# Squared-ReLU attention with a mixture-of-depths layer behind it: the table that orders all instructions is drawn anew

## The chip, the core and the metric

The kernel runs on one core of a Trainium2 chip. The metric is device time in microseconds (us) of one execution; lower is better.

## What is computed

For 8 batches, 12 heads, 448 tokens and head dimension 64, attention without softmax, and on its output a layer in which only 128 tokens of each batch pass through a two-matrix network:

```
scores = (1/sqrt(64)) * q @ k^T
attn   = max(scores, 0)^2 / 448
x      = attn @ v                      # as [8, 448, 768]
score  = x @ w_gate                    # one number a token
top    = the 128 tokens of a batch with the largest score
h      = max(x[top] @ w1, 0)           # 768 -> 1024
y      = h @ w2                        # 1024 -> 768
out    = x;  out[top] = x[top] + sigmoid(score[top]) * y
```

Inputs and output are float32 in DRAM; the matmuls run in bf16.

## The kernel before

**Units.** The attention of a batch is cut into three units of four heads; unit u belongs to batch u // 3, so there are 24 units, 0 to 23. Each unit has seven chunks c of 64 key rows. The second layer goes batch by batch, 0 to 7.

**The order is a table.** The kernel is written as short steps, each a function that issues one to 28 instructions. A string, ORDER (from line 518), lists some 1280 steps by name and numbers; a loop calls them in that order (the lines behind `with tc.manual_schedule()`). Every engine keeps its own queue and runs its instructions in the order in which they were issued; between engines, semaphores hold an instruction until what it reads is there and what it overwrites is free. So the table sets the order on each engine. An engine whose next instruction has to wait holds all that stands behind it in its own queue. A scheduling program drew the table up; it is not part of the kernel.

**Attention steps.** L,i,b,hh,j0,j1 (line 99) loads part of q, k or v (i = 0, 1, 2) of batch b from DRAM, for one half hh of the heads, converting to bf16, and is issued by POOL. There are three buffers for each of q, k and v, used by batches in turn. Batch 0 is loaded in parts (j0 to j1) and, for its first two head pairs, through float32 tiles (qf and kf, line 95) that C turns into bf16. T,u,i (229) transposes unit u's q or k on PE; TE,u copies both from PSUM into qkT. T0, TE0, SH, RH and QH are the same for unit 0 in halves. S,u,c (292) is four matmuls that make the scores of a chunk; R,u,c is the ReLU out of PSUM into a_sb, of which nearly all run on ACT (167 at line 114); Q,u,g (305) squares a group of chunks on DVE; V,u,c (313) is four matmuls that multiply with v. X,u scales the unit's result into xT_sb, on ACT or DVE.

**Steps of the second layer, for batch b.** G and CE make token scores, BC and RK compare every score with every other, CS and RC add up ranks, HOT and SEL turn ranks into a list of tokens, SE writes that list (idx). XR transposes x back on PE and XE evicts it into rows; for batches 5 and 6 XD (430) does this with DMA transposes that SP issues, each as soon as its unit's X is done. ST,b (434) stores rows to DRAM. GA,b (440) gathers the chosen tokens from there, once ST,b has landed; XT and XTE transpose them. For batches 0 and 7 XO and XOE pick them by matmul instead, and GA's rows are used only at the end. GS and SG make the gate. H,b,f (487) and HE are the first matrix, Y (499) and YE (507) the second with the final sum into the tile fo (two buffers), FI,b (512) scatters fo to DRAM. W,0 and W,1 load the two weight matrices.

**Where an engine is chosen.** The last letter of TE, R, X, XE, XTE, XOE, HE and C names it, A for ACT and D for DVE; `put` (line 112) issues the eviction there, so many rows of the profile share lines 114 (ACT), 116, 118 and 120 (DVE).

**POOL's queue.** POOL issues every load of a batch, the stores, gathers and scatters. P,u (192) is a one-element copy of unit u's qkT: it holds POOL until that unit is transposed, so that loads behind it wait until a buffer is free. GA holds POOL until the list is there, FI until fo is. N is a tiny memset ahead of some gathers and scatters. SP's queue holds the XD steps alone, in the middle of the program.

**Fillers.** WU (127) and WS (136) are matmuls on a tile of ones whose results nobody reads.

Of the kernel before, what the change touches and what calls it, by code (L numbers as in the profile page):

```python
# [20 lines left out]
def kernel(  # L21
# [497 lines left out]
    Z,9 Z,7 Z,3 Z,4 Z,6 Z,1 Z,2 L,1,0,1,2,4 L,0,0,1,2,4 L,1,0,0,2,4 C,0,0,A C,1,0,A L,0,0,0,2,4 WU,10,7,3 T0,0,0,4  # L519
    T0,1,0,5 L,1,1,1,0,6 TE0,0,0,4,A C,0,1,D L,0,0,0,4,6 TE0,1,0,5,A WU,1,7,3 T0,0,1,6 C,1,1,D Z,8 L,1,0,0,4,6 Z,10  # L520
    TE0,0,1,6,A WG WU,3,7,3 SH,1,0,0 L,1,0,1,4,6 T0,1,1,4 SH,0,0,1 L,0,0,1,4,6 TE0,1,1,4,D SH,2,0,2 SH,3,0,3
    RH,0,0,1,D RH,1,0,0,A L,0,1,0,0,6 WS,1,6 SH,0,1,4 RH,2,0,2,A RH,3,0,3,D T,1,0,6 L,0,1,1,0,6 RH,0,1,4,A S,0,4,0
    T,1,1,7 L,1,1,0,0,6 R,0,4,0,A S,0,5,2 TE,1,2,6,D S,0,6,4 L,2,0,1,0,2 R,0,5,2,A SH,3,1,0 L,2,0,0,0,2 RH,3,1,0,D
    R,0,6,4,A WU,2,1,3 S,1,0,2 L,2,0,1,2,4 QH,1,0,2 WS,1,6 S,1,1,0 R,1,0,2,A QH,0,0,2 WS,1,6 SH,2,1,4 L,2,0,0,2,4
    RH,2,1,4,D R,1,1,0,A WU,2,7,3 S,1,2,2 Q,0,2,3 T,2,0,6 R,1,2,2,A S,1,3,4 S,1,4,0 T,2,1,7 R,1,3,4,A Z,5 SH,1,1,2
    TE,2,2,6,D R,1,4,0,A WU,1,3,4 S,1,5,4 R,1,5,4,A RH,1,1,2,D P,2 WU,2,3,3 S,1,6,0 L,0,2,1,0,6 QH,1,1,2 WS,2,6
    S,2,0,2 R,1,6,0,A L,2,0,1,4,6 S,2,1,4 QH,0,1,2 T,3,0,6 R,2,0,2,A Q,1,0,3 WU,2,7,3 T,3,1,7 R,2,1,4,A S,2,2,0
    S,2,3,2 TE,3,2,6,D R,2,2,0,A V,0,0,4,1,0 V,0,1,4,0,0 R,2,3,2,A S,2,4,0 Q,2,0,3 P,3 L,2,0,0,4,6 T,4,0,6 T,4,1,7
    R,2,4,0,A L,0,2,0,0,6 S,2,5,2 V,0,2,4,0,0 TE,4,2,6,D L,1,2,1,0,6 R,2,5,2,A S,2,6,0 V,0,3,4,0,0 V,0,4,4,0,0
    L,1,2,0,0,6 V,0,5,4,0,0 R,2,6,0,A V,0,6,4,0,1 Q,1,1,4 S,3,0,2 L,2,1,1,0,6 T,5,0,6 R,3,0,2,A S,3,1,0 L,2,1,0,0,6  # L530
    T,5,1,7 R,3,1,0,A S,3,2,2 TE,5,2,6,D R,3,2,2,A S,3,3,0 Q,2,1,4 P,5 R,3,3,0,A W,1,6,8 S,3,4,2 V,1,0,6,1,0
    V,1,1,6,0,0 W,0,4,6 V,1,2,6,0,0 X,0,2,4,A V,1,3,6,0,0 V,1,4,6,0,0 V,1,5,6,0,0 L,0,3,1,0,6 S,3,5,0 R,3,4,2,A
    V,1,6,6,0,1 Q,3,0,3 V,2,0,4,1,0 V,2,1,4,0,0 V,2,2,4,0,0 R,3,5,0,A V,2,3,4,0,0 S,3,6,2 X,1,2,6,D R,3,6,2,A S,4,0,0
# [158 lines left out]
```

## Time and profile before

| | |
|---|---|
| three runs | 213.47, 213.60, 213.68 us; median 213.6 |
| the profiled execution | 215.22 us |
| its span, first to last instruction | 213.1 us |
| mean granted TensorE clock | 0.968 |
| PE busy | 193.6 us (91%), 3177 matmuls |
| DVE busy | 170.8 us (80%) |
| ACT busy | 164.9 us (77%) |
| POOL busy | 91.7 us (43%) |
| DMA | 37.89 MB in 34335 packets, mean 178 GB/s |

The profile is one execution, some 1.6 us longer than the median of the runs. In its rows a line number and tile names stand for a step: `L292 PE MATMUL psum<-qkT` is S, `L114 ACT ACTIVATE a_sb<-psum` is R. In the order of time the first column is the start, the second the duration, both in us from the span's start; what stands in brackets is how long the engine had been idle and what ended that. "issue" there means that nothing the profile shows was waited for. A DMA's row has the median time from its issue to its landing.

### The profile page before, as it was taken

How to read it: one execution, taken by the hardware profiler on the slowest of the kernel's cores; microseconds unless marked ns; L12 is line 12 of the kernel's file. 1: busy time of each engine (PE TensorE's matmuls, PEld its weight loads, DVE VectorE, ACT ScalarE, POOL GpSimd, SP SyncE). 2: the span in 40 equal slices, each digit the busy share in tenths (PEclk: the TensorE clock that was granted, in tenths of full speed). 3: DMA queues.
4: the chain of work that ended last, by engine and by line, in shares of the span. 5: the costliest groups of instructions: out<-in, count | busy, mean ns of one | idle time of the engine just before them, and what ended most of it. 6: DMA issues, size and time to landing. Idle time of an engine off the chain costs nothing.

```text
span 213.1 us, 7252 instructions
## 1 busy us (share of the span) xinstructions
PE 193.6 (91%) x3177; PEld 123.9 (58%) x3177; DVE 170.8 (80%) x263; ACT 164.9 (77%) x209; POOL 91.7 (43%) x130
## 2 busy tenths in 40 slices
PE   6889979999999999999799999989599699999970
PEld 2545555556776557656466546755356475698940
DVE  1489999998999989969799998998369956985340
ACT  2989999999989988789799999989459678541100
POOL 7953671350667281625174297061070028035121
PEclk9999999999999999999999999999769969999996
DMA  5999999999499999999999959999989946629411
GB/s 152 141 179 202 151 184 205 209 282 195 49 307 217 278 143 183 340 170 139 187 288 195 179 95 141 162 127 155 285 117 264 103 80 154 218 27 343 118 77 74
DMA packets 34335, 37.89 MB, mean 178 GB/s; under 512 B 8960, under 2 KB 29440, under 8 KB 34304
## 3 DMA queue, kind: packets, MB, share of 16 engines
q0 software_dynamic: 26352, 34.94, 87.2%
q1 hardware_dynamic: 7632, 2.04, 11.1%
q10 hardware_dynamic: 320, 0.46, 0.8%
q8 instruction: 25, 0.41, 0.7%
q14 instruction: 6, 0.05, 0.1%
HBM read 42.47 MB, written 14.16 MB: 266 GB/s over the span
## 4 chain that ended last, share of the span: by engine, by line
PE 41%; DMA 21%; ACT 17%; issue 9%; POOL 8%; DVE 1%; POOLq 1%; ACTq 0%
ACT a_sb L114 15%; PE psum L292 10%; DMA v_sb<-in_v_dram 9%; PE psum L313 9%; DMA out_dram<-rows 7%; PE psum L487 6%; PE psum L229 5%; DMA k_sb<-in_k_dram 5%; PE psum L499 4%; POOL k_sb L99 2%; POOL q_sb L99 2%; PE psum L343 2%; PE psum L416 2%; PE psum L354 1%; ACT xT_sb L114 1%
## 5 line engine op out<-in xcount | busy, mean ns | idle before, releaser
L114 ACT ACTIVATE a_sb<-psum 128x896 bf16<-128x896 f32 (+1 forms) x167 | 142.2, 926 | 15.5 <-PE psum L292 13.2
L305 DVE TENSOR_TENSOR a_sb<-a_sb 128x2688 bf16<-128x2688 bf16 (+3 forms) x49 | 83.4, 1712 | 0.6 <-ACT a_sb L114 0.6
L292 PE MATMUL psum<-qkT 64*64 64x448 bf16 x656 | 60.2, 371 | 2.4 <-ACT a_sb L114 2.0
L313 PE MATMUL psum<-a_sb,v_sb 64*64 64x448 bf16 x672 | 45.6, 361 | 2.9 <-issue 2.4
L292 PEld LDWEIGHTS <-qkT 64*64 64x64 bf16 x656 | 21.1, 105 | 21.4 <-issue 12.3
L118 DVE COPY qkT<-psum 128x1792 bf16<-128x1792 bf16 (+1 forms) x24 | 25.6, 1068 | 9.1 <-PE psum L229 7.7
L440 POOL DMA_INDIRECT xe<-out_dram,idx x8 | 14.5, 1810 | 42.6 <-DVE idx L412 40.2
L313 PEld LDWEIGHTS <-v_sb 64*64 64x64 bf16 x672 | 20.8, 109 | 14.5 <-issue 5.5
L192 POOL COPY pace<-qkT 1x1 bf16<-1x1 bf16 x18 | 11.7, 650 | 36.7 <-DVE qkT L118 36.7
L487 PE MATMUL psum<-xeT,w_sb 128*128 128x128 bf16 x384 | 26.9, 223 | 0.0
L499 PE MATMUL psum<-w_sb,hT 128*128 128x384 bf16 x128 | 26.8, 328 | 0.0
L487 PEld LDWEIGHTS <-w_sb 128*128 128x128 bf16 x384 | 22.7, 99 | 2.6 <-issue 2.5
L434 POOL DMA_DIRECT2D out_dram<-rows x16 | 10.4, 654 | 21.7 <-DVE rows L118 16.1
L499 PEld LDWEIGHTS <-hT 128*128 128x128 bf16 x128 | 11.1, 97 | 9.5 <-issue 4.7
L512 POOL DMA_INDIRECT out_dram<-fo,idx x8 | 10.5, 1311 | 10.6 <-DVE fo L507 7.1
L114 ACT ACTIVATE xT_sb<-psum 128x896 bf16<-128x896 f32 x14 | 13.1, 935 | 2.4 <-PE psum L313 2.4
L229 PE MATMUL psum<-ident,k_sb 128*64 128x128 bf16 x322 | 13.2, 220 | 1.4 <-DMA k_sb<-in_k_dram 1.3
L99 POOL DMA_DIRECT2D v_sb<-in_v_dram x20 | 13.1, 667 | 3.2 <-DMA k_sb<-in_k_dram 2.1
L229 PE MATMUL psum<-ident,q_sb 128*64 128x128 bf16 x322 | 13.5, 224 | 0.9 <-DMA q_sb<-in_q_dram 0.9
L229 PEld LDWEIGHTS <-q_sb 128*64 128x64 bf16 x322 | 9.9, 111 | 7.0 <-issue 6.0
L507 DVE SCALAR_TENSOR_TENSOR fo<-psum,g,xe 128x384 f32<-128x384 f32 x16 | 9.7, 615 | 4.8 <-ACT g L483 2.0
L120 DVE TENSOR_SCALAR xT_sb<-psum 128x896 bf16<-128x896 f32 x10 | 10.9, 1088 | 2.9 <-PE psum L313 2.6
(84 smaller groups left out, 205.4 us busy)
## 6 DMA issues: line engine op xcount, KB each, us to landing
out_dram<-rows POOLq DMA_DIRECT2D x8, 768.0 KB, 6.6
k_sb<-in_k_dram POOLq DMA_DIRECT2D x14, 336.0 KB, 7.4
q_sb<-in_q_dram POOLq DMA_DIRECT2D x14, 336.0 KB, 8.5
v_sb<-in_v_dram POOLq DMA_DIRECT2D x14, 336.0 KB, 9.0
out_dram<-rows POOLq DMA_DIRECT2D x8, 576.0 KB, 7.1
w_sb<-in_moe_w_dram POOLq DMA_DIRECT2D x4, 384.0 KB, 8.5
w_sb<-in_moe_w_dram POOLq DMA_DIRECT2D x3, 512.0 KB, 8.1
v_sb<-in_v_dram POOLq DMA_DIRECT2D x6, 112.0 KB, 7.7
```

Of the source, the lines that this page charges most:

```text
L99: nc.gpsimd.dma_start(out=qkv_sb[i][b % NBUF][64 * hh:64 * hh + 64, j0:j1], in_=srcs[i][b, NJ * hh + j0:NJ * hh + j1].rearrange("h (p c) d ...
L114: nc.scalar.activation(out=out_, in_=in_, func=func or AF.Copy, scale=scale)
L118: nc.vector.tensor_copy(out=out_, in_=in_)
L120: nc.vector.tensor_scalar(out=out_, in0=in_, scalar1=scale, scalar2=None, op0=ALU.mult)
L192: nc.gpsimd.tensor_copy(out=pace, in_=qkT[u][0:1, 1, 1, NC - 1, 63:64])
L229: nc.tensor.matmul(out=psum16[64 * j2:64 * j2 + 64, at, c * 128:(c + 1) * 128], lhsT=t[:, 2 * w + j2, c, :], rhs=ident, is_transpose=True, ...
L292: nc.tensor.matmul(out=psum[64 * hh:64 * hh + 64, at + j2, :S].rearrange("x (c p) -> x c p", c=NC), lhsT=sb[rows, hh, 1, c, :], rhs=sb[row ...
L305: nc.vector.tensor_tensor(out=a, in0=a, in1=a, op=ALU.mult)
L313: nc.tensor.matmul(out=psum[64 * j2:64 * j2 + 64, at + hh, :S], lhsT=qkv_sb[2][b % NBUF][rows, 2 * w + j2, c, :], rhs=a_sb[u, g][rows, i, ...
L440: inst = nc.gpsimd.indirect_dma_start(out=self.xe, out_offset=None, in_=out[0:self.b + 1].rearrange("b s d -> (b s) d"), in_offset=bass.In ...
L487: nc.tensor.matmul(out=psum[:, at, sub * CAP:(sub + 1) * CAP], lhsT=w1_sb[:, m, f * 128:(f + 1) * 128], rhs=self.xeT[:, m, :], start=(sub ...
L499: nc.tensor.matmul(out=psum[:, at, 0:384], lhsT=self.hT[:, f, :], rhs=w2_sb[:, f, half * 384:half * 384 + 384], start=bool(first), stop=bo ...
```

## The change

ORDER alone is replaced: 1284 steps become 1280. All functions, tiles and buffers stay, and so do all steps of computation, loads, stores, gathers and scatters. What differs is the order of steps, the PSUM banks that they use, the engine of some evictions, and fillers: N stands four times instead of seven, WU makes 28 matmuls instead of 29, WS 52 instead of 24. TE0 goes from three on ACT and one on DVE to four on DVE, HE from seven on ACT and nine on DVE to 13 and 3, X from 14 and 10 to 16 and 8.

Two lines of the table before, and those that hold the same steps after (XD,5 of batch 5 and what stands around it):

```diff
-    R,17,4,2,A V,15,6,4,0,1 S,17,5,0 XT,3,5 L,0,7,1,0,6 X,15,2,6,D R,17,5,0,A Y,2,0,6,4,0,0
-    Y,2,0,7,4,0,1 S,17,6,2 R,17,6,2,A S,18,0,0 XTE,3,5,D XD,5,0,0 T,19,0,6 YE,2,0,4,D T,19,1,7 R,18,0,0,A S,18,1,2
...
+    V,15,3,4,0,0 S,17,6,2 V,15,4,4,0,0 V,15,5,4,0,0 R,17,6,2,A XT,3,6 XE,4,1,7,D S,18,0,0 V,15,6,4,0,1 XTE,3,6,D
+    R,18,0,0,A S,18,1,2 X,15,2,4,D T,19,0,6 R,18,1,2,A T,19,1,7 S,18,2,0 XD,5,0,0 TE,19,2,6,D V,16,0,4,1,0
```

**ACT, the start of the program.** Before, from the casts C of batch 0 on (q_sb and k_sb; qkT is TE0, a_sb of 448 is RH, of 896 R):

```order
L114 ACTIVATE q_sb_83<-qf 128x448
L114 ACTIVATE k_sb_86<-kf 128x448
L114 ACTIVATE qkT<-psum 64x7x2x64 x3
L114 ACTIVATE a_sb<-psum 128x448 x3
L114 ACTIVATE a_sb<-psum 128x896 x21
```

After, the same place:

```order
L114 ACTIVATE k_sb_86<-kf 128x448
L114 ACTIVATE q_sb_83<-qf 128x448
L114 ACTIVATE k_sb_86<-kf 128x448
L114 ACTIVATE a_sb<-psum 128x448 x2
L114 ACTIVATE a_sb<-psum 128x896 x28
```

The three TE0 have left ACT, a cast has come, one RH has left, and 28 R steps instead of 21 stand ahead of the first X.

**POOL, from GA,3 to the v load of batch 7.** In the names v_sb_89, q_sb_83 and k_sb_86 are the buffers of batch 6, q_sb_84, k_sb_87 and v_sb_90 those of batch 7; rows of xe are GA, of out_dram from rows ST,4, of out_dram from fo FI (896x768 is FI,1), and pace from qkT is P. Before:

```order
L440 DMA xe<-out_dram,idx 128x768
L205 MEMSET pace 1x1
L512 DMA out_dram<-fo,idx 896x768
L192 COPY pace<-qkT 1x1
L99 DMA q_sb_84<-in_q_dram 64x6x448
L192 COPY pace<-qkT 1x1
L99 DMA k_sb_87<-in_k_dram 64x6x448 x2
L99 DMA v_sb_89<-in_v_dram 64x6x448
L99 DMA q_sb_84<-in_q_dram 64x6x448
L434 DMA out_dram<-rows 64x4x768
L434 DMA out_dram<-rows 64x3x768
```

After:

```order
L440 DMA xe<-out_dram,idx 128x768
L99 DMA v_sb_89<-in_v_dram 64x6x448
L99 DMA q_sb_84<-in_q_dram 64x6x448
L99 DMA v_sb_89<-in_v_dram 64x6x448
L192 COPY pace<-qkT 1x1
L99 DMA k_sb_87<-in_k_dram 64x6x448 x2
L434 DMA out_dram<-rows 64x3x768
L434 DMA out_dram<-rows 64x4x768
L512 DMA out_dram<-fo,idx 896x768
```

FI,1 has moved from right behind GA,3 to behind ST,4. Two loads that stood behind P,18 (the last P here), one of v for batch 6 and one of q for batch 7, now stand ahead of it. The first q load of batch 7 now goes out ahead of GA,3, and a v load of batch 6 that went out ahead of it now follows it. All these loads are of the same size.

**ACT, the end of the attention.** Before, from the last but one pair of R steps on (xT_sb is X, g is SG, rows is XE,7):

```order
L114 ACTIVATE a_sb<-psum 128x896 x2
L114 ACTIVATE xT_sb_93<-psum 128x2x448
L114 ACTIVATE a_sb<-psum 128x896
L483 ACTIVATE g<-psum 128x1
L114 ACTIVATE rows<-psum 128x768 x3
```

After:

```order
L114 ACTIVATE a_sb<-psum 128x896 x4
L114 ACTIVATE xT_sb_93<-psum 128x2x448
L114 ACTIVATE a_sb<-psum 128x896 x2
L114 ACTIVATE xT_sb_93<-psum 128x2x448 x2
L114 ACTIVATE rows<-psum 128x768 x3
```

X,22 and X,23 now both stand behind the last R step on ACT; before, X,22 stood ahead of the last R and X,23 on DVE.

More of the change, by code (lines that the diff above doesn't have):

```diff
@@ L518 @@
     ORDER = """
[L519 to L533, printed above, removed]
@@ new lines @@
+    L,1,0,0,4,6 T0,1,0,5 TE0,0,0,4,D L,0,0,0,4,6 C,0,1,A TE0,1,0,5,D C,1,1,A L,0,1,0,0,6 WU,2,7,3 T0,0,1,4 TE0,0,1,4,D
+    WU,1,7,1 T0,1,1,5 L,0,0,1,4,6 SH,1,0,0 TE0,1,1,5,D SH,0,0,1 SH,2,0,2 L,1,0,1,4,6 RH,0,0,1,D RH,1,0,0,A WS,1,6
+    T,1,0,6 RH,2,0,2,A L,2,0,1,0,2 SH,3,0,3 S,0,4,0 S,0,5,4 RH,3,0,3,D L,0,1,1,0,6 R,0,4,0,A T,1,1,7 L,1,1,0,0,6
+    SH,3,1,2 TE,1,2,6,D R,0,5,4,A S,0,6,0 SH,2,1,3 L,2,0,0,0,2 R,0,6,0,A RH,2,1,3,D S,1,0,4 L,1,1,1,0,6 Z,5 R,1,0,4,A
+    L,2,0,1,4,6 WS,4,6 S,1,1,0 RH,3,1,2,D R,1,1,0,A QH,1,1,2 WS,4,6 S,1,2,2 S,1,3,4 T,2,0,6 Q,0,2,3 R,1,2,2,A S,1,4,0
@@ new lines @@
+    V,4,1,6,0,0 Q,5,1,4 R,6,1,2,A G,0,4,5,0,0 S,6,2,0 V,4,2,6,0,0 V,4,3,6,0,0 R,6,2,0,A G,0,5,5,0,1 S,6,3,2
+    V,4,4,6,0,0 V,4,5,6,0,0 V,4,6,6,0,1 R,6,3,2,A S,6,4,0 CE,0,5 X,4,2,6,D T,7,0,4 R,6,4,0,A T,7,1,5 S,6,5,2
+    TE,7,2,4,D BC,0,6 R,6,5,2,A S,6,6,0 RK,0,3,6 R,6,6,0,A V,5,0,4,1,0 P,7 RK,0,2,6 W,1,4,6 V,5,1,4,0,0 S,7,0,2
+    RK,0,1,6 V,5,2,4,0,0 V,5,3,4,0,0 R,7,0,2,A W,1,0,2 RK,0,0,6 V,5,4,4,0,0 S,7,1,0 V,5,5,4,0,0 L,2,2,0,0,6 Q,6,1,4
+    V,5,6,4,0,1 R,7,1,0,A S,7,2,2 T,8,0,6 X,5,2,4,A T,8,1,7 S,7,3,0 R,7,2,2,A TE,8,2,6,D CS,0,4 XR,1,3,5 R,7,3,0,A
@@ new lines @@
+    XR,2,0,7 R,10,4,2,A XE,2,1,5,D G,2,1,4,0,0 S,10,5,0 XR,2,3,6 R,10,5,0,A XR,2,2,5 XE,2,3,6,D G,2,2,4,0,0
+    G,2,3,4,0,0 G,2,4,4,0,0 G,2,5,4,0,1 S,10,6,2 CE,2,4 XE,2,2,5,D R,10,6,2,A WU,2,1,4 XT,1,6 S,11,0,0 XTE,1,6,D
+    S,11,1,4 S,11,2,2 R,11,0,0,A XE,2,0,7,D H,1,0,6,0 Q,10,1,4 H,1,1,6,1 R,11,1,4,A ST,2,1 H,1,2,6,2 H,1,3,6,3 ST,2,0
+    R,11,2,2,A H,1,4,4,0 S,11,3,0 P,11 L,0,5,1,0,6 HE,1,0,6,A BC,2,5 Q,10,0,3 R,11,3,0,A H,1,5,4,1 P,10 L,2,4,1,0,6
+    S,11,4,2 T,12,0,6 R,11,4,2,A T,12,1,7 RK,2,3,5 RK,2,2,5 S,11,5,0 TE,12,2,6,D H,1,6,4,2 R,11,5,0,A S,11,6,2
@@ new lines @@
+    BC,3,6 S,15,1,2 R,15,0,0,A HE,2,0,7,D T,16,0,4 T,16,1,5 RK,3,3,6 R,15,1,2,A RK,3,2,6 S,15,2,0 RK,3,1,6 H,2,4,7,0
+    R,15,2,0,A RK,3,0,6 S,15,3,2 H,2,5,7,1 TE,16,2,4,D R,15,3,2,A H,2,6,7,2 S,15,4,0 GS,2,6 R,15,4,0,A H,2,7,7,3
+    Q,14,1,4 P,16 S,15,5,2 L,1,6,1,0,6 V,13,0,4,1,0 V,13,1,4,0,0 R,15,5,2,A S,15,6,0 L,0,6,0,0,6 V,13,2,4,0,0
+    V,13,3,4,0,0 V,13,4,4,0,0 SG,2,6 R,15,6,0,A V,13,5,4,0,0 L,0,6,1,0,6 S,16,0,2 HE,2,1,7,D CS,3,6 V,13,6,4,0,1
+    R,16,0,2,A S,16,1,0 RC,3,6 X,13,2,4,D T,17,0,6 R,16,1,0,A T,17,1,7 HOT,3 S,16,2,2 V,14,0,4,1,0 TE,17,2,6,D
@@ new lines @@
+    V,14,1,4,0,0 R,16,2,2,A V,14,2,4,0,0 S,16,3,0 V,14,3,4,0,0 V,14,4,4,0,0 R,16,3,0,A Q,15,0,3 S,16,4,2 P,17
+    V,14,5,4,0,0 L,0,7,0,0,6 SEL,3,6 R,16,4,2,A Y,2,0,0,7,1,0 S,16,5,0 Y,2,0,1,7,0,0 V,14,6,4,0,1 SE,3,6 R,16,5,0,A
+    Q,15,1,4 S,16,6,2 GA,3 Y,2,1,0,6,1,0 Y,2,1,1,6,0,0 Y,2,0,2,7,0,0 R,16,6,2,A Y,2,0,3,7,0,0 S,17,0,0 Y,2,1,2,6,0,0
+    Y,2,1,3,6,0,0 R,17,0,0,A Y,2,0,4,7,0,0 Y,2,0,5,7,0,0 Q,16,1,4 L,2,6,0,0,6 Y,2,0,6,7,0,0 Y,2,0,7,7,0,1
+    Y,2,1,4,6,0,0 X,14,2,4,A S,17,1,0 L,0,7,1,0,6 S,17,2,2 Y,2,1,5,6,0,0 R,17,1,0,A L,2,6,1,0,6 T,18,0,4 T,18,1,5
@@ L639 @@
+    Y,7,0,2,4,0,0 Y,6,0,4,6,0,0 Y,6,0,5,6,0,0 Y,6,0,6,6,0,0 Y,6,0,7,6,0,1 Y,7,0,3,4,0,0 Y,7,1,0,5,1,0 YE,6,0,6,D
+    Y,7,0,4,4,0,0 Y,7,0,5,4,0,0 Y,7,0,6,4,0,0 GS,7,7 N FI,6 Y,7,0,7,4,0,1 Y,7,1,1,5,0,0 SG,7,7 Y,7,1,2,5,0,0
+    YE,7,0,4,D Y,7,1,3,5,0,0 Y,7,1,4,5,0,0 Y,7,1,5,5,0,0 Y,7,1,6,5,0,0 Y,7,1,7,5,0,1 YE,7,1,5,D N FI,7
     """
```

193 lines of the change are left out of this document (89 added, 104 removed).

## The prediction

> **What bounds the kernel now.** I read the page first, then the stretches of the span that its slices suggested, then the order of time where an engine stood still, and the DMA view of those places last. In the stretches each engine's busy time stands with its instruction count, then the granted TensorE clock and the DMA share:
>
> ```profile
> 21.00:50.80 29.80, 27.31 (x490) 16.10 (x491) 29.08 (x34) 29.69 (x38) 12.68 (x19) 1.00 1.17 205
> 50.80:130.70 79.90, 78.01 (x1363) 49.88 (x1356) 73.53 (x100) 72.15 (x92) 41.53 (x53) 1.00 1.05 196
> 130.70:150.00 19.30, 18.66 (x339) 12.45 (x339) 17.87 (x25) 18.20 (x24) 5.85 (x9) 1.00 1.43 151
> 150.00:160.00 10.00, 7.52 (x107) 4.17 (x105) 4.66 (x8) 5.14 (x7) 4.05 (x4) 0.66 1.03 195
> ...
> 175.70:184.10 8.40, 8.40 (x128) 4.94 (x128) 6.51 (x15) 7.67 (x10) 4.48 (x5) 1.00 0.83 232
> 184.10:206.60 22.50, 22.40 (x338) 18.27 (x330) 13.37 (x33) 3.89 (x8) 6.69 (x11) 1.00 0.44 122
> ```
>
> The columns are PE, PEld, DVE, ACT, POOL. From 21 to 50.8 us ACT is the bound (29.69 of 29.8). To 150 three engines share it: PE, DVE and ACT are each busy over 90%. From 184.1 to 206.6 PE alone works through the experts of the last batches (22.40 of 22.5). A last eviction, a scatter and its landing follow. One place stands out: from 150 to 160 ACT worked 5.14 of 10 us and the clock fell to 0.66. The order of time shows what happened, on PE and then on ACT:
>
> ```profile
> 149.86 0.21 PE L343 MATMUL psum<-wg,xT_sb 128*128 128x1 bf16 x3
> 152.56 0.54 PE L343 MATMUL psum<-wg,xT_sb 128*128 128x1 bf16 x15 [2.48 <-issue]
> 167.57 1.29 PE L313 MATMUL psum<-a_sb,v_sb 64*64 64x448 bf16 x21
> 170.64 0.38 PE L313 MATMUL psum<-a_sb,v_sb 64*64 64x448 bf16 x3 [1.77 <-issue]
> ...
> 153.66 1.97 ACT L114 ACTIVATE a_sb<-psum 128x896 bf16<-128x896 f32 x2 [2.73 <-PE psum L292]
> 156.27 0.92 ACT L114 ACTIVATE a_sb<-psum 128x896 bf16<-128x896 f32 x1 [0.64 <-PE psum L292]
> 157.70 0.92 ACT L114 ACTIVATE a_sb<-psum 128x896 bf16<-128x896 f32 x1 [0.52 <-PE psum L292]
> 159.46 4.16 ACT L114 ACTIVATE a_sb<-psum 128x896 bf16<-128x896 f32 x5 [0.84 <-PE psum L292]
> 171.06 0.92 ACT L114 ACTIVATE xT_sb<-psum 128x896 bf16<-128x896 f32 x1 [1.86 <-PE psum L313]
> ...
> 178.20 1.73 ACT L114 ACTIVATE a_sb<-psum 128x896 bf16<-128x896 f32 x2 [0.69 <-PE psum L292]
> ```
>
> PE twice stopped for "issue", that is, for nothing that the profile shows, and both times in the middle of a step: three matmuls into a G step of four, and one into a V step of four, whose data the first had already found. No data wait does that. ACT's idle time behind the first stop is 2.73 + 0.64 + 0.52 + 0.84 = 4.7 us, behind the second at least 1.86 + 0.69 = 2.6 us: 7.3 us in all. The DMA view explains the stops. Its first row is of the whole run, the second of 150 to 151.5 us, then median landing times of 80 to 120 us, and of 127 to 150 us:
>
> ```profile
> q8 instruction: 25, 0.41, 0.7%
> ...
> q8 instruction: 1, 0.02, 4.5%
> ...
> v_sb<-in_v_dram POOLq DMA_DIRECT2D x5, 336.0 KB, 8.7
> ...
> v_sb<-in_v_dram POOLq DMA_DIRECT2D x2, 336.0 KB, 13.0
> rows<-xT_sb SPq DMA_TRANSPOSE x6, 12.3
> out_dram<-fo,idx POOLq DMA_INDIRECT x1, 13.7
> ```
>
> PE's instructions come by DMA. The page counts 3177 matmuls and as many weight loads; over 25 packets that is 254 instructions each. The view of 140.4 to 150 us has no q8 row. In those 9.6 us PE ran, at the 678 instructions of 19.3 us above, some 337, more than a packet holds; a packet came in the next 1.5 us and PE went on. So PE ran dry, because its packet stood behind the transposes, loads, stores and scatter that took 12 to 14 us to land there. [...]
>
> **The change, part by part.** Work is the same; only order, banks and a few evictions' engines differ. All terms are against the profiled execution.
>
> *The head.* The rows are PE's first transposes, the cast of q's second half behind its landing, ACT's and DVE's first evictions to qkT, and the first double-width R:
>
> ```profile
> 5.91 0.58 PE L258 MATMUL psum<-ident,q_sb 128*64 128x128 bf16 x7 [1.45 <-ACT q_sb L114]
> 6.73 0.39 DVE L118 CAST q_sb<-qf 128x448 bf16<-128x448 f32 x1 [4.87 <-DMA qf<-in_q_dram]
> 6.52 2.65 ACT L114 ACTIVATE qkT<-psum 64x896 bf16<-64x896 bf16 x3 [0.20 <-PE psum L258]
> 9.28 0.63 DVE L118 COPY qkT<-psum 64x896 bf16<-64x896 bf16 x1 [1.18 <-PE psum L258]
> 11.55 4.98 ACT L114 ACTIVATE a_sb<-psum 128x896 bf16<-128x896 f32 x6 [0.63 <-PE psum L292]
> ```
>
> Three TE0, 2.65 us on ACT, go to DVE at 0.63 each, 1.9 us. The first two start near 6.4 as before and end near 7.6 instead of 8.3; the second half's casts (now on ACT, from 6.73) let the other two end near 9.2 instead of 9.9. Two RH instead of three stand on ACT ahead of its R steps, and S,0,4 is ready near 9.8: the first R comes near 10.3 instead of 11.55. Then ACT has R steps queued until unit 1, whose k half is landed by then. Up to 50.8 us ACT is the bound, so the lead stays. I take -1.1 us (0 to -1.4; 0 if unit 1's transposes still wait for their k loads).
>
> *The middle, 50.8 to 184.* Between R,6,6 and R,23,6 ACT gets two HE more (8 for 6) and DVE two fewer.
>
> ```profile
> L116 DVE TENSOR_SCALAR hT<-psum 128x512 bf16<-128x512 f32 x9 | 6.1, 687 | 4.7 <-PE psum L487 4.7
> L114 ACT ACTIVATE hT<-psum 128x512 bf16<-128x512 f32 x7 | 4.2, 600 | 4.9 <-PE psum L487 4.8
> ```
>
> That is 2 x 0.60 = +1.2 us on ACT and 2 x 0.69 = -1.4 on DVE. Each is busy about 90% there, so it costs between -1.4 and +1.2; I take +0.6, since ACT is what the late R steps wait for. Loads and T steps move against each other by one or two R in both directions; there I take 0, with 1.0 either way.
>
> *The congested stretch, 127 to 175.* POOL's rows show the burst in order of time; the last two rows are an X eviction and the transposes (XD) that SP issues as soon as it is done:
>
> ```profile
> 125.08 1.83 POOL L512 DMA_INDIRECT out_dram<-fo,idx  x1 [0.23 <-issue]
> 127.04 0.69 POOL L99 DMA_DIRECT2D q_sb<-in_q_dram  x1
> 131.39 0.69 POOL L99 DMA_DIRECT2D q_sb<-in_q_dram  x1
> 139.97 1.27 POOL L434 DMA_DIRECT2D out_dram<-rows  x2 [7.89 <-DVE rows L118]
> 142.59 2.07 POOL L512 DMA_INDIRECT out_dram<-fo,idx  x1 [0.30 <-issue]
> ...
> 158.07 1.09 DVE L120 TENSOR_SCALAR xT_sb<-psum 128x896 bf16<-128x896 f32 x1 [1.84 <-PE psum L313]
> 159.19 15.31 SPq L430 DMA_TRANSPOSE rows<-xT_sb  x6
> ```
>
> 158.07 + 1.09 = 159.16, and SP issues at 159.19: XD goes when X is done. Before, FI,1 (the 125.08) sits ahead of five loads that go out from 127.0 to 132.1. After, FI,1 stands behind ST,4, and three of the five loads go right behind GA,3 without waiting for P,18: about 1.5 us earlier. X,15 follows R,18,0 instead of R,17,4, X,16 R,18,4 instead of R,18,2, X,17 R,19,4 instead of R,19,3; with R steps of some 0.85 us (4.98 for six) the transposes go 2.6, 1.7 and 0.9 us later. ST,4 and the v load go 1 to 3 us later too. What went into the queues in 15.6 us (127.0 to 142.6) thus takes about 19. Counted along PE's order, its packet falls due at the same step as before, at S,19,2, with 3 to 4 us less ahead of it. It was late by the 2.48 us that PE stood still. So the stop should vanish or shrink to some tenths, and the clock stay up: I take -4.2 of the 4.7 us (0 to -4.7). At the second stop the same transfers are ahead (two ST,5, a v load, XD,6), now with FI,2 among them; ST,5 waits for the later XD,5, so one packet may pass ahead of them and the next not. I take half, -1.3 us (+1 to -2.6).
>
> [...]
>
> *The tail.* The rows: V steps, an XT, an X on ACT and the last X on DVE.
>
> ```profile
> 180.80 1.50 PE L313 MATMUL psum<-a_sb,v_sb 64*64 64x448 bf16 x28
> 183.09 0.50 PE L449 MATMUL psum<-ident,xe 128*128 128x128 bf16 x6
> 179.81 0.93 ACT L114 ACTIVATE xT_sb<-psum 128x896 bf16<-128x896 f32 x1
> 186.16 1.09 DVE L120 TENSOR_SCALAR xT_sb<-psum 128x896 bf16<-128x896 f32 x1 [0.40 <-PE psum L313]
> ```
>
> After R,23,6 PE is the bound to the end, so what is left to it then counts in full. Two V steps more (2 x 0.21) and one XT more (0.35 of 0.50, pipelined) are left: +0.8. Before, GS and two H steps covered most of X,23; after, only the seven small matmuls of CS stand between V,23,6 and G, and X,23 goes to ACT, at the 0.93 of xT_sb's rows there (179.81): PE waits some 0.6 us. I take +1.4 (+0.5 to +2).
>
> Sum: -1.1 + 0.6 + 0 - 4.2 - 1.3 + 1.4 = -4.6. The span is 213.1 us and the execution 215.2, 2.1 around it; so 215.2 - 4.6 = 210.6. The three runs have a median of 213.6, 1.6 below this execution. If the difference is longer stops under the profiler, the gain is smaller by that and the time still 210.6; if it is spread evenly, 213.6 - 4.6 = 209.0. Stops that depend on DMA traffic are the likelier place; I forecast 210.4.
>
> **The rivals.**
>
> *The packet still comes too late.* The transfers are the same in number, XD,5 and ST,4 still stand ahead of the request, and 254 instructions are all the reserve. If the packet lands later than those 254 instructions after S,19,2, PE stops as before and the clock falls. Then only head, middle and tail are left: -1.1 + 0.6 + 1.4 = +0.9, 214.5 us, slower. For it: unchanged volume. Against: 3 to 4 us more room where 2.48 were missing. Chance 0.18.
>
> *The backlog does not set the packet's wait.* If the packet waits its turn, but not behind all that was queued earlier, then room ahead of it buys nothing: the transposes are in flight at S,19,2 before and after, and the stops stay with them, at the same +0.9 and 214.5 us. Against it stand the 9.6 us without a packet. Chance 0.07. [...]
>
> *The scatter takes its place.* FI,1 now queues behind XD,5 and ST,4; its landing took 13.7 us for its successor there. YE,3,0 writes a buffer that FI,1 reads (two buffers), so DVE waits in YE,3,0 and holds TE,22 and the Q steps behind it. FI,1 goes out about 20 us later than its 125.08, near 143; landing by 157 against a YE,3,0 near 153 costs up to 4 us of DVE, perhaps 1.5 of the end: 211.9, faster still. Chance 0.15.
>
> *The change does nothing there, or only the second stop stays and the head lead is lost to DMA:* 213.6, no change. Chance 0.06.
>
> **How the numbers follow.** The forecast has 0.54, its own range 207.6 to 212.4 (unknown ends of the head, middle and second stop, about 2 us either way). Two runs of this kernel can be told apart from about 0.2%, 0.4 us. Faster: 0.54 + 0.15 = 0.69, less 0.02 for a wait of over 3.5 us in the scatter case: 0.67. Same 0.07, slower 0.26. The range, to leave out 2 in 10, reaches from 207.6 to the first rival's 214.5.
>
> **What would show it.** Right: no "issue" gap of PE over 1 us between 135 and 175, the clock at 1.0 there, R's first at about 10.3, X,23 followed by a short PE gap. Wrong: a q8 packet missing for over 9 us again with a stop of PE in mid-step; DVE's YE,3,0 ended by the scatter; or ACT or PE gaps in 50 to 130 us that grow by more than 2 us.

## The result, and the profile after

| us | before | after |
|---|---|---|
| executions | 212.03, 213.47, 213.60, 213.68 | 206.64, 206.81, 207.52, 209.93 |
| median | 213.53 | 207.17 |
| profiled execution (span) | 215.22 (213.1) | 206.64 (204.8) |

The ratio of after to before is 0.9709, 95% interval 0.9649 to 0.9769. The forecast was 210.4 in 207.6 to 214.5: the direction held, the time lies 0.4 us below the range. The comparison leaves out executions over 1.5% above the fastest of their kernel (here the 209.93); so on the later chips, where about half of before's executions are that much longer, a ratio is against its shorter executions alone, which are taken below as stop-free by their time, not by a trace.

After, in stretches, with the columns as before:

```profile
50.60:130.70 80.10, 79.69 (x1399) 51.30 (x1390) 73.64 (x104) 74.35 (x95) 43.77 (x52) 1.00 1.08 205
...
140.00:150.00 10.00, 10.00 (x174) 5.55 (x162) 9.42 (x18) 9.33 (x13) 3.59 (x6) 1.00 1.16 229
150.00:160.00 10.00, 10.00 (x182) 6.09 (x179) 9.18 (x17) 9.79 (x13) 4.70 (x5) 1.00 1.11 134
160.00:170.00 10.00, 10.00 (x181) 6.97 (x182) 9.78 (x14) 9.11 (x13) 1.93 (x2) 1.00 1.11 194
...
174.10:198.10 24.00, 23.26 (x349) 18.95 (x341) 9.45 (x25) 8.25 (x16) 7.46 (x12) 1.00 0.47 135
```

From 150 to 160 us PE is busy 10.00 of 10 us at clock 1.00; before it was 7.52 at 0.66. From 50.6 to 174 PE is busy 99.5 to 100%: it alone is the bound there, as far as the modelled ends of its matmuls tell. Its whole list of waits holds no "issue" any more:

```profile
PE psum L292 <- ACT a_sb L114: 1.3, 4, 0.4
PE psum L258 <- DVE q_sb L118: 1.1, 1, 1.1
PE psum L127 <- DVE warm L108: 1.1, 1, 1.1
PE psum L416 <- ACT xT_sb L114: 0.7, 1, 0.7
```

(The columns are us in all, times, longest.) Matching the rows with the table of order gives the end of each R step, and so where the 8.4 us of the span went. The third column is b_split, a form of before in which no stop fell (below):

| end of | before | after | b_split | after minus before, by stretch |
|---|---|---|---|---|
| R,6,6 | 50.83 | 50.60 | 51.14 | -0.2 |
| R,20,3 | 150.12 | 147.96 | 147.47 | -1.9 |
| R,21,3 | 161.19 | 154.53 | 153.52 | -4.5 (first stop) |
| R,23,6 | 184.08 | 174.10 | 173.12 | -3.3 (second stop) |
| span | 213.1 | 204.8 | 202.2 | +1.6 (tail) |

### The profile page after: what moved, and what is told of

The parts are those of the page before. It is cut to its first block, busy times and chain, and to the rows that moved or that the text cites. A ratio compares the mean times of both kernels' runs of the same rounds, so it can differ in the third digit from the quotient of the medians.

```text
span 204.8 us, 7305 instructions
## 1 busy us (share of the span) xinstructions
PE 191.4 (94%) x3204; PEld 124.7 (61%) x3204; DVE 168.1 (82%) x257; ACT 166.3 (81%) x215; POOL 93.6 (46%) x127
## 4 chain that ended last, share of the span: by engine, by line
PE 71%; DVE 8%; ACT 8%; issue 6%; DMA 2%; POOL 1%; POOLq 1%; SPq 0%; DVEq 0%; ACTq 0%
PE psum L292 17%; PE psum L313 13%; PE psum L487 9%; PE psum L499 8%; PE psum L229 8%; ACT a_sb L114 7%; PE psum L416 4%; DVE a_sb L305 3%; DVE qkT L118 3%; PE psum L343 2%; DMA qf<-in_q_dram 2%; PE psum L354 2%; PE psum L465 2%; PE psum L127 2%; PE psum L258 1%
## 5 line engine op out<-in xcount | busy, mean ns | idle before, releaser
L114 ACT ACTIVATE a_sb<-psum 128x896 bf16<-128x896 f32 (+1 forms) x166 | 140.7, 932 | 10.4 <-PE psum L292 5.9
L292 PE MATMUL psum<-qkT 64*64 64x448 bf16 x656 | 58.9, 364 | 2.0 <-ACT a_sb L114 1.3
L313 PE MATMUL psum<-a_sb,v_sb 64*64 64x448 bf16 x672 | 44.3, 352 | 0.3 <-ACT xT_sb L114 0.2
L292 PEld LDWEIGHTS <-qkT 64*64 64x64 bf16 x656 | 22.1, 104 | 20.6 <-issue 9.9
L118 DVE COPY qkT<-psum 128x1792 bf16<-128x1792 bf16 (+1 forms) x27 | 27.5, 1021 | 4.6 <-PE psum L258 2.0
L192 POOL COPY pace<-qkT 1x1 bf16<-1x1 bf16 x18 | 15.1, 838 | 33.4 <-DVE qkT L118 31.4
L440 POOL DMA_INDIRECT xe<-out_dram,idx x8 | 13.5, 1682 | 30.0 <-DVE idx L412 15.3
L487 PEld LDWEIGHTS <-w_sb 128*128 128x128 bf16 x384 | 22.0, 97 | 4.5 <-issue 4.2
L114 ACT ACTIVATE xT_sb<-psum 128x896 bf16<-128x896 f32 x16 | 14.9, 930 | 0.3 <-PE psum L313 0.3
L114 ACT ACTIVATE hT<-psum 128x512 bf16<-128x512 f32 x13 | 7.7, 615 | 6.5 <-PE psum L487 6.5
```

Of the source, the lines that this page charges most:

```text
L114: nc.scalar.activation(out=out_, in_=in_, func=func or AF.Copy, scale=scale)
L118: nc.vector.tensor_copy(out=out_, in_=in_)
L192: nc.gpsimd.tensor_copy(out=pace, in_=qkT[u][0:1, 1, 1, NC - 1, 63:64])
L292: nc.tensor.matmul(out=psum[64 * hh:64 * hh + 64, at + j2, :S].rearrange("x (c p) -> x c p", c=NC), lhsT=sb[rows, hh, 1, c, :], rhs=sb[row ...
L313: nc.tensor.matmul(out=psum[64 * j2:64 * j2 + 64, at + hh, :S], lhsT=qkv_sb[2][b % NBUF][rows, 2 * w + j2, c, :], rhs=a_sb[u, g][rows, i, ...
L440: inst = nc.gpsimd.indirect_dma_start(out=self.xe, out_offset=None, in_=out[0:self.b + 1].rearrange("b s d -> (b s) d"), in_offset=bass.In ...
```

## The experiments

Of the eighteen runs sixteen change before (b_) or after (a_) in the steps shown; after_again and after_ref are after unchanged. Executions of one kernel scatter by several us, so each run is told by its profile, which is one execution, and by how many executions took over 209 us. Of the 97 executions of before on six chips 48 did (4 of 4 on the first, 3 of 7, 14 of 29, 10 of 23, 9 of 17, 8 of 17 on the others); the rest lie at 204.6 to 209. Of after's 28, one did.

### Moving the packets' borders alone: b_split, a_split

```diff
 def WU(n, at, w):
+    n, w = n * w, 1
     for _ in range(n):
```

> The kernel before with each filler matmul of 384 or 512 columns written as three or four of 128: the same columns, 60 matmuls and 60 weight loads more on PE's queue, all ahead of 100 us. Packet theory: PE's packets hold 256 instructions, so all packet borders move 120 instructions (some 3.4 us of work) towards the start of the program. A stop for issue can then not stand in batch 5's G step, nor in unit 19's V step; the packet is asked for at about 139 instead of 142.5 us, among the transposes, and a stop of 0 to 2.5 us may come some 60 matmuls earlier. Time 210 to 214. Rival, the stop belongs to its step or to the data there: PE stops 2.5 us in batch 5's G step and 1.8 us in unit 19's V step as before, clock 0.97, 213.6 us.

> The kernel after with the same edit, 46 matmuls and 46 weight loads more. Packet theory with less backlog: the longest wait of a packet after the change left over 60 instructions in hand, so at another phase stops are 0 to 1 us and the time 207 to 208.5. Rival, the new order only moved the borders to a lucky place: a stop of 2 us or more comes back and the clock falls, 210 us or more. Rival, the stop was never a matter of packets: no change, 207.2.

b_split: 204.17, 204.31, 208.28, 208.43, ratio 0.9896 (0.9839 to 0.9953), faster than either theory expected. No stop in its profile, with before's transfers untouched. a_split: 205.81 to 210.01, ratio 1.0045 (0.995 to 1.0141), and a stop of 1.16 us where after had none, between what the two theories expected. Here it is, on PE, with two more from later runs, b_pool and b_pool_split:

```profile
165.81 0.28 PE L488 MATMUL psum<-xeT,w_sb 128*128 128x128 bf16 x2
167.25 0.33 PE L488 MATMUL psum<-xeT,w_sb 128*128 128x128 bf16 x3 [1.16 <-issue]
```

```profile
162.98 1.29 PE L313 MATMUL psum<-a_sb,v_sb 64*64 64x448 bf16 x21
165.23 0.38 PE L313 MATMUL psum<-a_sb,v_sb 64*64 64x448 bf16 x3 [0.95 <-issue]
```

```profile
152.73 0.30 PE L230 MATMUL psum<-ident,q_sb 128*64 128x128 bf16 x4
155.37 0.47 PE L230 MATMUL psum<-ident,q_sb 128*64 128x128 bf16 x10 [2.35 <-issue]
```

All in mid-step, in an H, a V and a T step. Count the recorded instructions of PE's queue from the start of the program (matmuls, weight loads, and its few semaphore and drain instructions; 6378 in before), each as one entry. The first matmul behind a stop then has 4545, 4801 and 5313 entries ahead of it (before), 5569 (a_split, a_xd, a_head), 5313 (b_pool), 5057 (b_pool_split, b_v7) and 4801 (a_v7). Modulo 256 each of these is 193, and so is every other idle time of PE over 0.06 us that the twenty profiles put down to "issue", 19 in all. Each profile has 25 such places in PE's list, and 25 packets of 16 KB. So a stop belongs to a packet's border, not to a step or its data: shown.

### POOL's order alone: b_pool, a_pool, a_pool_again

The steps of POOL in b_pool (a_pool moves after's steps the other way round):

```diff
 GA,3
-N FI,1
...
+L,2,6,1,0,6 L,0,7,1,0,6
 P,18
...
-L,2,6,1,0,6
...
-L,0,7,1,0,6
...
 ST,4,1
+N FI,1
```

> The kernel before with POOL's order of after in one stretch: FI,1 behind ST,4 and two loads (v of batch 6, q of batch 7) ahead of the last P. PE's list is unchanged. If it is POOL's order that made room: the first stop shrinks from 2.5 to under 0.7 us, the time falls to 209 to 211. If the transposes that go out later are what made room: FI,1 still stands ahead of the packet that is asked for near 142.5, the stop stays at 1.5 to 3.5 us, and YE,3,0 of batch 3 waits for FI,1's buffer, up to 4 us on DVE: 213 to 216.

> The kernel after with POOL's order of before in that stretch: FI,1 right behind GA,3, and three loads behind the last P and behind both k loads. PE's list is unchanged. If POOL's order made room: a stop of 1.5 us or more comes back near 140 to 150 us and the time is 209.5 or more. If the later transposes made room: no stop over 0.7 us, 206.8 to 208.

> Once more the kernel after with POOL's order of before in the stretch around GA,3. If POOL's place of FI,1 and the two loads is what keeps after free of stops, a third or more of the executions take 209 us or more; if not, nearly all lie at 205 to 208.5 like those of after.

b_pool: 205.07, 205.62, 206.37 and 208.46, ratio 0.9966 (0.9909 to 1.0023); the first stop is gone, the second 0.95 us in the 208.46 execution, which is the profiled one. a_pool: 205.01 to 206.80, no stop over 0.31 us; a_pool_again: median 207.31, 2 of 12 over 209, ratio 1.0036 (0.9994 to 1.0079). POOL's order thus took the first stop out of before's one profile here (none of 4 executions over 209, against 3 of 7 of before beside it, which is few), and after mostly does without it. YE,3,0 did not wait for FI,1 in after nor in b_pool: the scatter rival did not come.

### More traffic on purpose: after_again, a_loads, a_xd, b_pool_split

DL is a load of v, DX a transpose, each into a spare tile; a_loads, then a_xd:

```diff
 L,1,7,1,0,6
+DL,0,0 DL,0,1 DL,1,0
```

```diff
 XD,5,1,1
+DX,0 DX,3 DX,1 DX,4
```

> The kernel after, unchanged, beside the kernel before on one chip. Packet theory: executions of before fall into two groups, 205 to 207 us without a stop and 212 to 213.5 with the stops; the new order leaves the packet 60 instructions or more in hand, so after lies at 206 to 208 in nearly all executions, and where before happens not to stop, after is no faster than it (its tail is 1.4 us longer): 206 to 207 against 206. Rival, the gain is in the order's other parts: after is faster than the stop-free executions of before too, by 2 us or more.

> The kernel after with three loads more (336 KB each, of v, into a tile that nobody reads), on POOL behind the last k load of batch 7, ahead of the packet that PE asks for near 139 us. Nothing on PE's queue changes. Packet theory, all DMA traffic alike: each load adds about 2 to 3 us of queue, the packet comes 4 to 8 us later, PE stops 2 to 5 us at the border near 146 us and the clock falls: 211 to 215 us. Rival, only the transposes hold packets up: no stop over 0.5 us there; some us may be lost to later k loads and stores, 207 to 209.

> The kernel after with four DMA transposes more on SP's queue behind XD,5,1,1 (of the same units, into a tile that nobody reads), issued from about 137.5 us. PE's and POOL's queues are unchanged. Packet theory: with the transposes of batch 5 then ten instead of six, the packet asked for near 139 us comes 3 to 6 us later and PE stops 1 to 4 us at the border near 146 us: 209 to 213 us. Rival, the transposes cost the packet nothing: no stop over 0.5 us, 207 to 208.

> The kernel before with both edits that were tried singly: FI,1 behind ST,4 with two loads earlier, and the fillers written as matmuls of 128 columns (120 instructions more). Packet theory: borders and traffic no longer meet, no stop over 1 us in nearly all executions, 204 to 205.5 us, faster than after by 1 to 2 us since head, middle and tail are before's. Rival, one of the edits only had luck: stops in half of the executions, 205 to 209.

after_again: 206.50 to 208.68 in 12 executions, 0.9992 of before's stop-free ones (0.9964 to 1.0021): beside the stops the change makes nothing faster that this comparison can tell. a_loads: median 213.09, but by data waits, not by a packet. PE's border is at 140.3 us; these are the DMA views of a_loads from 140.5 to 143.9 and from 143.9 to 145:

```profile
q0 software_dynamic: 601, 0.52, 92.4%
q1 hardware_dynamic: 595, 0.14, 32.8%
...
rows<-xT_sb SPq DMA_TRANSPOSE x1, 17.1
```

```profile
q0 software_dynamic: 178, 0.16, 98.3%
...
q8 instruction: 1, 0.02, 5.8%
```

The transpose of the first view was issued at 138.3 us, ahead of the border, and took 17.1 us to land, at 155.4; the packet set out 3.6 us after the border, at 143.9. So it does not stand behind all that was queued before it, and this theory, the prediction's, falls in that form. But loads ahead of a border do cost it time. At this border the seven profiles of after's order whose loads there are untouched (after, after_again, after_ref, a_he, a_head, a_split, a_xd) show waits of 1.1 to 1.9 us; the four that add loads ahead of it or move loads nearer to it (a_loads, a_pool, a_pool_again and, below, a_v7) show 3.6 to 4.6. Four transposes more do not hold the packet (a_xd: waits of 1.1 and 3.2 us near them; a stop of 1.17 us came later, beside a v load; median 208.64, 4 of 10 over 209). b_pool_split: ratio 0.9969 (0.993 to 1.0007), 5 of 12 over 209, with the stop of 2.35 us above. Two edits, each with fewer stops than before, bring one back together; it looks as if what decides is which border meets which moment.

### Without transposes, and without stores: b_noxd, b_nost

b_noxd leaves out the twelve XD; four groups like this one stand for them:

```diff
-XD,5,0,0
...
+XR,5,0,4 XR,5,1,5 XE,5,0,4,A XE,5,1,5,D
```

b_nost:

```diff
-ST,4,0
-ST,4,1
-ST,5,0
-ST,5,1
...
 FI,3
+ST,4,0 ST,4,1 ST,5,0 ST,5,1
```

> The kernel before without DMA transposes: the rows of batches 5 and 6 are made by XR on PE and XE on ACT and DVE, as for the other batches (48 matmuls and 8 evictions more, 12 transposes fewer on SP; PE's list is the same up to 149 us). Theory that the transposes hold the packet up: no wait of a packet over 4.5 us from 130 us on, no stop, and no execution over 209; the median is about 3 us above the stop-free executions of before for the added PE work, 208 to 210. Theory that the stores do it: waits of 6 to 9 us and stops stay in half of the executions, which then take 213 or more.

> The kernel before with the four stores of rows of batches 4 and 5 moved from 140 to 160 us to the end of the attention (about 177 us), and the gathers of these two batches reading batch 0 instead, so that the second layer of batches 4 and 5 works on other rows. Transposes, loads and PE's list stay. Theory that the stores hold the packet up (in the traces the waits over 5 us nearly all have a store or a scatter in flight beside transposes): no wait over 4.5 us, no stop, 205 to 207 us in nearly all executions. Theory that the transposes do it: waits and stops as before, executions of 209 to 214 in about half.

b_noxd: no packet waited over 3.0 us from 130 us on, no stop, clock 0.99 in all six executions, so none stood at half clock as long as before does behind its first stop; the added PE work and evictions cost more than thought (212.05 to 215.27). b_nost: waits to 4.5 us, no stop in the attention, which is what the theory of the stores expected, not that of the transposes; but this is one profile. The stores at 175 us held GA,6 up, PE stood 3.72 us for it, and the time (210.96 to 213.53) tells nothing of packets. So neither run rules the other's theory out.

### Evictions' engines: a_he

```diff
-HE,0,0,6,A  HE,1,0,6,A  HE,2,0,7,D  HE,3,0,7,A
+HE,0,0,6,D  HE,1,0,6,D  HE,2,0,7,A  HE,3,0,7,D
```

> The kernel after with four HE back on the engines of before (HE,0,0, HE,1,0 and HE,3,0 on DVE, HE,2,0 on ACT). The prediction's term: two HE fewer on ACT give 0.6 us back, within -1.2 to +1.4. Rival, PE is the only bound from 50 us on (it is 99 to 100% busy wherever no packet is late): no change, within 0.3 us, between R,6,6 and R,23,6 of the profile.

Median 208.60, ratio 1.0077 (1.0032 to 1.0122). From R,6,6 to R,23,6 its profile takes 125.3 us, after_again's 123.7, after's 123.5 and after_ref's 124.8: 0.5 to 1.8 slower, never 0.6 faster, where after's own order differs by 1.3 among its profiles.

### Loads: b_early, a_head, after_ref, a_best

POOL's steps in b_early, then at the start of a_head; a_best has both kinds of move:

```diff
+L,0,7,0,0,6 L,0,7,1,0,6 L,1,7,0,0,6 L,1,7,1,0,6 L,2,6,1,0,6
 GA,3 N FI,1
+L,2,7,0,0,6 L,2,7,1,0,6
...
-L,0,7,0,0,6 L,1,7,1,0,6 L,1,7,0,0,6 L,2,6,1,0,6 L,0,7,1,0,6
...
-L,2,7,0,0,6 L,2,7,1,0,6
```

```diff
-L,0,1,0,0,6
 L,0,0,1,4,6 L,1,0,1,4,6
-L,2,0,1,0,2
+L,0,1,0,0,6
 L,0,1,1,0,6 L,1,1,0,0,6
-L,2,0,0,0,2
 L,1,1,1,0,6
+L,2,0,1,0,2 L,2,0,0,0,2
```

> The kernel before with the loads of 127 to 160 us moved ahead: five of batches 6 and 7 to about 118 us, ahead of GA,3, and the two v loads of batch 7 behind FI,1 at about 127. Transposes, stores and PE's list are unchanged. Theory that long waits of PE's packet take transposes and loads in flight together: waits from 134 us on stay under 4.5 us, no stop, 204.5 to 206.5 us and few executions over 209. Theory that transposes alone do it: a wait of 5 us or more and stops as before, a third or more of the executions over 209.

> The kernel after with POOL's first loads in another order: the second and later q and k loads of batch 1 ahead of the first v loads, and the first q load of batch 1 behind the last q and k loads of batch 0. Theory that the head's lead is lost to loads: the waits of PE at 15 to 20 us (T,2 and T,3, 0.7 to 2.6 us in all) fall below 0.5, R,2,6 ends about 1 us earlier (24.5 against 25.3 to 26.5), and the end with it: 206 against 207.3. Rival, the lead is taken back by ACT or by later loads before 50 us: R,6,6 and the end unchanged, within 0.4 us.

> The kernel after once more, for the comparison on this chip: 206.5 to 208.5 us, with at most one execution in ten over 209.

> The kernel after with both edits, the loads of the start as in the run before and the loads of batches 6 and 7 ahead of GA,3 or right behind it. If both theories hold: 205 to 206.5 us, faster than after on the same chip by 0.5 us or more, and no execution over 209. If only the start helps: as that run. If the earlier loads hold up GA,3 or each other: 207 to 208.5.

after_ref: 206.38 to 208.45 in 12. b_early: 213.07 to 215.90, since the moved loads delayed another; its waits on PE:

```profile
PE psum L313 <- DMA v_sb<-in_v_dram: 6.0, 2, 5.5
```

Its packets from 132 us on waited 0 to 3.3 us, and none stopped PE. a_head: 1.0111 (1.0073 to 1.0149), slower than after beside it (after_ref's 1.0053). The wait for T,2, 1.18 us in after_ref, went, and two others remained or came:

```profile
18.15 0.58 PE L229 MATMUL psum<-ident,q_sb 128*64 128x128 bf16 x14 [0.80 <-DMA q_sb<-in_q_dram]
...
22.58 0.76 PE L313 MATMUL psum<-a_sb,v_sb 64*64 64x448 bf16 x12 [1.70 <-DMA v_sb<-in_v_dram]
```

V,0 now waits for the v load that was put back: every early load is needed when it comes. a_best: 216.11 to 219.47; GA,3 queued behind the moved loads and PE stood 6.9 us for it.

### Two loads alone: b_v7, a_v7

b_v7 (a_v7 has them behind L,1,7,1,0,6):

```diff
 L,0,7,1,0,6
+L,2,7,0,0,6 L,2,7,1,0,6
...
-L,2,7,0,0,6
...
-L,2,7,1,0,6
```

> The kernel before with the two v loads of batch 7 moved from 141.6 and 158.2 us to about 132, right behind the last q load of batch 7; all else unchanged, PE's list too. Theory that long waits take loads and transposes together: the wait at the border near 160 us falls under 4.5 us and the second stop is gone; the first one stays possible, since two loads more are in flight there, so a third of the executions are still over 209, but fewer over 212; time without stops 205 to 207. Theory that the transposes alone do it: waits of 5 us or more at the border near 160 us too, half of the executions over 209.

> The kernel after with the same two loads moved behind the last k load of batch 7 (from 140 and 154 us to about 129). Loads and transposes together: the wait at the border near 162 us falls from 2.8 to 5.2 us to under 2.5, no stop there; that near 140 us grows by up to 2 us, without a stop; 206 to 207.5, no execution over 209. Transposes alone: the wait near 162 us unchanged; 207 to 208.5.

b_v7: 205.42 to 208.79, median 206.89, none of 12 over 209, while before beside it had 8 of 17. Two steps of the old table, moved, are worth about what the new table is worth; against before's stop-free executions it is 1.0047 (1.0008 to 1.0085), so like after it beats before only by its stops. At the border where before's packet for the second stop was asked for, the wait is 2.7 us in place of 6.6; one stop of 0.89 us remained, behind a wait of 5.5 us at the border ahead of that, where a moved v load was in flight. The same move in after (a_v7) brought a stop: 205.52 once, and 209.32 to 216.69 five times. PE in a_v7:

```profile
146.48 0.18 PE L372 MATMUL psum<-low,ones 128*128 128x4 bf16 x1
150.48 0.29 PE L377 MATMUL psum<-minus,g_sb 128*128 128x1 bf16 x6 [3.83 <-issue]
```

And its DMA from 144.3 to 148.0 us:

```profile
DMA packets 386, 0.25 MB, mean 69 GB/s; under 512 B 323, under 2 KB 330, under 8 KB 386
...
q1 hardware_dynamic: 321, 0.08, 123.4%
q0 software_dynamic: 65, 0.18, 103.7%
...
rows<-xT_sb SPq DMA_TRANSPOSE x2, 11.9
```

The packet set out at 144.2 and took 3.96 us, against 0.9 elsewhere; in those 3.7 us all 16 engines moved 69 GB/s, against 199 GB/s of after's 127 to 150 us. Before, from 140 to 142 us, around the border at 141.5 us where the packet for the first stop was asked for, looks alike:

```profile
DMA packets 102, 0.07 MB, mean 37 GB/s; under 512 B 51, under 2 KB 101, under 8 KB 101
...
q0 software_dynamic: 53, 0.04, 81.2%
q1 hardware_dynamic: 48, 0.01, 68.0%
```

But there it lasts half a microsecond of the packet's wait: from 142 to 146 us the engines moved 156 GB/s, and the packet set out only at 150.14, 8.65 us after the border. And a_split, which has a stop of 1.16 us, has no such slow microsecond between 128 and 172 us. So slow engines fit the packet of a_v7, and not before's.

### Every packet's wait

From the last entry that PE starts ahead of a border to the start of the packet of that border, in all twenty profiles between 20 and 175 us, by what was in flight (where a landing is not recorded, 9 us after its issue are taken; "stores" are ST and FI):

| in flight at the border | packets | mean wait, us | 5 us or more | longest |
|---|---|---|---|---|
| no transpose, no store | 172 | 2.3 | 0 | 4.3 |
| no transpose, stores | 138 | 2.6 | 7 | 5.9 |
| transposes, no load, no store | 18 | 1.1 | 0 | 3.6 |
| transposes, no load, stores | 29 | 2.0 | 1 | 8.4 |
| transposes and loads, no store | 27 | 3.3 | 1 | 5.8 |
| transposes, loads and stores | 31 | 4.3 | 10 | 8.7 |

The seven without a transpose are one border of after's order, near 59 us; stops of at most 0.44 us stand behind them. The 8.4 is in a_v7, at the border where it stood 3.83 us; from the end of that stop it is 4.4. So 18 of the 19 long waits have a store in flight, 18 have a load and 12 have a transpose, and those over 6 us have transposes and stores. Most packets take 0.9 to 1.6 us, PE goes on 1.2 to 2.3 us after the packet has landed, and 256 entries last some 7 us; so, as an estimate from these, a wait of about 5 us begins to stop it (in before a wait of 4.0 us stood ahead of 0.11 us of idle time, one of 5.8 us ahead of the 0.62).

## Why the prediction was right or wrong

**The stops: right in place and direction, half right in why, and the second mis-sized.** "So PE ran dry, because its packet stood behind": that PE ran dry at packet borders is shown. That the packet stood behind the whole backlog fell with a_loads, where it overtook a transpose. The rival that it waits its turn was right in that, and wrong twice: that "room ahead of it buys nothing", since two or three loads added or moved there go with waits 2 to 3 us longer in the four profiles above (in two of them FI,1 was moved too), and that "the stops stay with them", the transposes, since after had one execution in 28 over 209. Waits like the 8.65 us of before stand where transposes, loads and stores fly together (10 of the 19 of 5 us or more); why they are so long is not shown. "3 to 4 us less ahead of it" thus pointed the right way (1.5 us in after at that border, for 8.65), but is not what safety from stops hangs on: the new order moved borders and transfers so that they miss each other, and a_split and a_v7 show how little brings them together again.

First stop: -4.2 forecast, -4.5 measured. Second: "I take half, -1.3", measured -3.3. Half was the chance that one packet passes; the stop went whole. And its price was read off ACT's idle rows (2.6 us), which miss what PE does slowly: the granted clock was 0.50 for 6.8 us from 151.5 us, around the first stop's end, and for 3.4 from 172.0, behind the second (0.66 over 10 us in the prediction's first rows, and 0.89 over the 15.7 us behind them, a row that it does not show). Stop plus half of that is 2.48 + 3.4 = 5.9 and 1.77 + 1.7 = 3.5; the second is near the 3.3 measured, the first is more than the 4.5.

**The middle: +0.6 forecast, -1.9 measured, wrong bound.** "Three engines share it" was read from busy shares over 90%. Without late DMA PE is busy 99.5% or more, so HE on ACT or DVE cannot give 0.6: a_he took two back and did not gain. Before's own execution lost time there that the order didn't ask for, on PE by a late k load of batch 5 and by a third, small stop at a border (entry 4545), which the prediction overlooked:

```profile
104.86 0.58 PE L229 MATMUL psum<-ident,k_sb 128*64 128x128 bf16 x14 [1.15 <-DMA k_sb<-in_k_dram]
...
142.46 0.76 PE L313 MATMUL psum<-a_sb,v_sb 64*64 64x448 bf16 x12 [0.62 <-issue]
```

From R,6,6 to R,20,3 before takes 99.3 us and b_split 96.3, of which 1.6 lie at the first row (R,13,6 to R,14,6) and 0.8 about the second (R,16,6 to R,20,3). After takes 97.4. So the order cost about +1, and before's late loads and small stop -3; the "0, with 1.0 either way" didn't hold them.

**The head: -1.1 forecast, -0.2 measured in this pair.** "The first R comes near 10.3": in after it came at 11.68, since PE's full clock was granted only from 9.0 us and the first seven transposes, at 5.87, took 0.95 us (0.58 at 9.24). In a_split, with the clock up in time, the same order gives it at 10.39. ACT, in after and then in a_split:

```profile
10.17 0.98 ACT L114 ACTIVATE a_sb<-psum 128x448 bf16<-128x448 f32 x2 [2.27 <-PE psum L272]
11.68 1.73 ACT L114 ACTIVATE a_sb<-psum 128x896 bf16<-128x896 f32 x2 [0.53 <-PE psum L292]
```

```profile
8.88 0.98 ACT L114 ACTIVATE a_sb<-psum 128x448 bf16<-128x448 f32 x2 [1.18 <-PE psum L273]
10.39 1.73 ACT L114 ACTIVATE a_sb<-psum 128x896 bf16<-128x896 f32 x2 [0.53 <-PE psum L293]
```

There PE then waited 2.10 us for unit 2's q load, the forecast's "0 if unit 1's transposes still wait", one unit further on:

```profile
16.27 0.58 PE L230 MATMUL psum<-ident,q_sb 128*64 128x128 bf16 x14 [2.10 <-DMA q_sb<-in_q_dram]
```

**The tail: +1.4 forecast, +1.6 measured, right by its terms.** PE's end minus R,23,6 is 24.0 us after and 22.4 before: PE is busy 23.26 against 22.40, so 0.9 of work for the 0.8 worked out, and idle 0.74 against 0.1 for the 0.6 forecast.

**Which time the sum is made from.** -4.6 against -8.4 in the span. "The time still 210.6" took the 1.6 us between the profiled execution and the median for longer stops under the profiler. The shorter executions on other chips suggest what a stop-free before takes, 204.6 to 209; by that estimate some 7 us of the 213.5 were stops and late loads, all of which the new order shed, while everything else in it together gains nothing: 0.9992 (0.9964 to 1.0021) and 1.0053 (1.0017 to 1.0088) beside such executions. Both stops going whole would not have left the range: at the prediction's own prices, -4.7 and -2.6, its sum is -6.4 and its time 208.8. The steps that failed are the middle, which had +0.6 where -1.9 came, and the price of the second stop, -1.3 where -3.3 came; the head's missing 0.9 takes back a part.

**Open.** Why packets at some borders wait 5 us or more and at others, with the same kinds of transfers in flight, 1, isn't settled. That before's long stops take transposes is made likely by b_noxd's six executions, though its list on PE differs from 149 us on; shorter stops came without. That they take loads or stores beside them rests on the table and on the borders of b_early, b_v7 and b_nost, where other things moved too, and no run parts loads from stores. One profile without a long wait proves little: b_split kept all of before's transfers, and its longest from 130 us on was 4.6 us. Why before stopped in every execution on the first chip and in about half on the others wasn't tried.

## What to carry to other kernels

A stop in mid-step with "issue" behind it can be an empty instruction queue: count PE's recorded instructions modulo 256 before blaming a step (193 at all 19 idle times here), and price it as the stop plus up to half of the time at half clock (3.5 for 3.3 measured here, 5.9 for 4.5). The clock need not be down right behind a stop: 0.3 us behind the end of b_pool_split's 2.35 us, 14 transposes took 0.58 us, as they do at full clock. A gain from removing such stops is a gain in how often they come, so compare many executions and on more than one chip. Before drawing a table anew, try to move a load or two off the borders that stop: two of 1284 steps did about as much here. Count executions after each such move, for it is no rule: the same two loads moved in the new table brought a stop of 3.83 us, and moving more of them made b_early and a_best wait for data.
